# Attention and feed-forward on one core: the scores of the first seven head pairs as float32 products over six PSUM banks, first loads on two queues, a refitted transfer model

## The chip, the cores and the metric

The kernel runs on one core of a Trainium2 chip. The metric is the device time of one execution in microseconds (us), the median of three runs. Engines are named as in the profile: PE (TensorE, matrix products), DVE (VectorE), ACT (ScalarE), POOL (GpSimd) and SP (the queue from which nearly all transfers are issued). Each engine works through its own instructions strictly in the order in which the program lists them.

## The reference

Attention over 4 batches, 12 heads, 448 positions of 64 values, with scores capped at 30·tanh(s/30); its output, 1792 tokens of 768 values, goes through a feed-forward layer of width 2048. The feed-forward weights are handed over as 64-bit numbers and decoded on the chip.

```python
scores = scale * np.matmul(q, k.transpose(0, 1, 3, 2))
scores = cap * np.tanh(scores / cap)
attn = np.exp(scores - max);  attn = attn / (sum + 1e-09)
x = np.matmul(attn, v)              # -> 1792 x 768
h = x @ w_in                        # 768 x 2048
out = (h - np.tanh(h)) @ w_out      # 2048 x 768
```

## The kernel before

**Order.** A planner (class Plan) takes every operation with an estimated cost, the operations that it depends on and a due time, and simulates the engines and the transfer queues; the order that comes out is written down once, and each engine then follows it. So a constant of the planner changes no instruction, but it changes where instructions stand. `LEAD` and the `..._LAG` numbers say how early loads may be issued, `LANES`, `ISSUE` and the factors `slow` say what a transfer costs in the simulation.

**Attention.** Heads are taken in 24 pairs (6 per batch). A load of q or k brings two pairs (four transfers, 112 KB each; the very first pair is loaded alone), a stream transpose on DVE (L560) makes `qT` and `kT`, with the first head of a pair on partitions 0 to 63 and the second on 64 to 127. The scores of a pair are seven blocks of 128x448 (three per head, and one "tail" block whose 128 rows hold the last 64 rows of both heads). For the first `TILED_PAIRS` = 8 pairs k and q are split into a high and a low fp32r part (k: cast on ACT, L453, and difference on DVE, L464; q: scaled by `s8` on ACT, L583, difference on DVE, L588), and a block is three fp32r products, high·high, high·low, low·high (L745): a "visit" of PE makes the blocks of both heads, six products of 64 rows each, alternating between the two halves of the array; the tail takes three products of 128 rows from `kt`. All eight heads after that use "stacked" products of 128 rows (L710, 15 to a pair). Then ACT takes tanh out of PSUM (L755 or L718) and exp (L810).

The probabilities are multiplied with v (PV): for the first 11 pairs as float32 products (L889, 8 to a pair), which leave two records each in the trace. They accumulate in two banks of tag `s`; the denominators come out with them. To free a bank, DVE transposes the sums (`fsumT`, L921) and the rows are copied (`fnum`, L453 on ACT or L455 on DVE). Between two visits PE takes two or three PV products of the pair before.

**Feed-forward.** Five segments of chunks f (128 rows of weights each). In the first two segments each chunk's 64-bit weights are loaded (`w64`: two transfers of 384 KB, one of 768 KB), decoded on DVE in three passes (L1076, L1083, L1090) and written back decoded by POOL's queue for later segments. PE: L1222 to L1224 and L1275.

Batch 0's attention runs alone (to about 62 us); from then on attention and feed-forward chunks alternate on PE. PSUM has eight banks: `acc0` to `acc4`, two `s`, `h`.

**Start.** SP issues the cap's load, then k and q of the first pair and k and q of the second. A warm-up of 18 products on zeros runs on PE (L486). ACT loads its table for tanh at once (L1573).

Of the kernel before, what the change touches and what calls it, by code (L numbers as in the profile page):

```python
# [37 lines left out]
LEAD = (18000.0, 40000.0, 30000.0, 30000.0, 30000.0)  # L38

FREE_PAIRS = 8  # L40

TILED_PAIRS = 8
# [3 lines left out]
INSPECT_LAG, RAW_LAG, KEPT_LAG, V_LAG, QK_LAG = 15000.0, 3000.0, 3000.0, 3000.0, 1000.0  # L46
# [9 lines left out]
START = (1700.0, 2000.0, 3300.0, 1060.0, 2300.0)  # L56
# [7 lines left out]
GROUP = 3 * SCORE + 400.0  # L64
SCORES = 3 * GROUP + 3 * SCORE

SHIFT = 110.0

LANES = 8


BANKS = ["acc0", "acc1", "acc2", "acc3", "acc4", "s", "s", "h"]
# [247 lines left out]
class Build:  # L320
# [6 lines left out]
    def __init__(self, ctx, tc, q, k, v, w_in, w_out, out, consts, checks, general):  # L327
# [40 lines left out]
        for i in range(self.plan.tags["kt"]):  # L368
            t = self.cst.tile([128, 2, 2, self.TAIL], F32R, name=f"{nm}kt{i}")
            nc.gpsimd.memset(t.bitcast(F32)[:D, :, 1, :], 0.0)  # L370
            nc.gpsimd.memset(t.bitcast(F32)[D:, :, 0, :], 0.0)
            self.fixed["kt"].append(t)
# [20 lines left out]
        if not general:  # L393
            self.least, self.flagf, self.flag = checks
# [77 lines left out]
    def dma(self, eng, nbytes, fn, deps=(), alloc=(), uses=(), slow=1, long=False, key=1e18, lag=0.0):  # L472
        c = (650.0 if long else 550.0) if eng == "SP" else 600.0
        return self.plan.op(eng, c, fn, deps, alloc, uses, key, dma=nbytes * slow / 360.0, lag=lag)
# [4 lines left out]
    def warm_up(self):  # L479
# [8 lines left out]
        o = self.plan.op("D", 300.0, lambda: nc.vector.memset(z().bitcast(F32), 0.0), [], [z], key=-1e6)  # L488
        self.plan.op("PE", COLS[384] * WARM, fn, [o], [P], [z], key=-1e6)
# [3 lines left out]
    def fetch_qk(self, b, p, np_):  # L493

        nc, S = self.nc, self.S
        for nm, src in (("k", self.k), ("q", self.q)):
            raw = self.plan.buf(nm + "raw", [128, 2, S // 32, 32])
            ops = []
            for i in range(4):
# [3 lines left out]
                def fn(i=i, h=h, dh=dh, raw=raw, src=src):  # L503
                    nc.sync.dma_start(  # L504
# [6 lines left out]
                        "SP", np_ * S * 128, fn, [], [] if ops else [raw], [raw] if ops else [], slow=2.3,  # L511
                        lag=QK_LAG if (b, p) > (0, 1) else 0.0,
# [8 lines left out]
    def fetch_v(self, b, p):  # L521
# [4 lines left out]
        for hp in range(2):  # L526
            src = self.v[b, p + self.NP * hp]
            full, tail = (src[0:FULL], src[FULL:]) if hp == 0 else (src[TAIL:], src[0:TAIL])
            for part in range(2):

                def fn(hp=hp, part=part, full=full, tail=tail):
# [5 lines left out]
                    else:  # L537
# [6 lines left out]
                        [vr] if ops else [], slow=1.8, long=True, lag=V_LAG if (b, p) > (0, 0) else 0.0,  # L544
# [4 lines left out]
    def prep_pair(self, b, p):  # L549
# [3 lines left out]
        nc, S, D, F, TL, plan = self.nc, self.S, self.D, self.FULL, self.TAIL, self.plan  # L553
        T, tr = {}, {}
        for nm in ("k", "q"):
            raw, j, ops = self.raw_qk.pop((nm, b, p))
            t = T[nm] = plan.buf(nm + "T", [128, S])
            tr[nm] = self.dve(
                S,
                lambda t=t, raw=raw, j=j: nc.vector.transpose(t(), raw()[:, j].rearrange("p j a -> p (j a)")),  # L560
                ops, [t], [raw], extra=28,
            )
        if not self.tiled(b, p):
            return self.stack_pair(b, p, T, tr)
        kst, kt, qst = plan.buf("kst"), plan.buf("kt"), plan.buf("qst", [128, 2, S], F32R)
        kops = list(
            self.split(
                S, lambda: kst()[:, :S], lambda: kst()[:, S + TL :], T["k"], [tr["k"]], ([kst], []),
                ([T["k"]], [kst, T["k"]]),
            )  # L570
        )
        tops = []
        for h, c0 in ((0, F), (1, 0)):
# [3 lines left out]
                    2 * TL, lambda h=h, rows=rows: kt()[rows, :, h, :],  # L577
                    lambda rows=rows, c0=c0: self.pieces(kst(), rows, c0), kops,
                    [] if h else [kt], [kst, kt] if h else [kst], half=True,
                )  # L580
            )
        o1 = self.act(
            S, lambda: nc.scalar.activation(qst()[:, 0, :], T["q"](), AF.Copy, scale=self.s8), [tr["q"]],  # L583
            [qst], [T["q"]], aps=1,
        )
        o2 = self.dve(
            S,
            lambda: nc.vector.scalar_tensor_tensor(  # L588
                qst()[:, 1, :], T["q"](), self.s8, qst()[:, 0, :].bitcast(F32), op0=ALU.mult, op1=ALU.subtract
            ),  # L590
            [o1], [], [qst, T["q"]], extra=60,
        )
        self.ready[b, p] = dict(kst=kst, kt=kt, qst=qst, kops=kops, tops=tops, qops=[o1, o2])

    def tiled(self, b, p):
        return b * self.NP + p < TILED_PAIRS

    def pieces(self, kst, rows, c0):

        S, TL = self.S, self.TAIL  # L600
        t = kst[rows, c0 : c0 + S + 2 * TL].bitcast(F32)
        return t.rearrange("p (a b) -> p a b", b=TL)[:, 0 : S // TL + 2 : S // TL + 1, :]
# [73 lines left out]
    def s_banks(self, b, p, n):  # L676

        at = b * self.NP + p
        tags = ["s"]
        if b == 0:  # L680
            tags = ["acc0", "acc1", "acc2", "acc3", "acc4"]
        elif at < FREE_PAIRS:
            tags = ["acc0", "acc1", "s", "s"]
        self.s_rr = getattr(self, "s_rr", -1)
        out = []
        for _ in range(n):
            self.s_rr += 1
            out.append(self.plan.buf(tags[self.s_rr % len(tags)]))
        return out

# [32 lines left out]
    PRODUCTS = ((0, 0), (0, 1), (1, 0))  # L723

    def qk_group(self, b, p, c, dsts, e):
# [3 lines left out]
        heads = 2 if c < 3 else 1  # L729
        if not self.tiled(b, p):  # L730
            made = [self.stacked_block(b, p, h, c, e, dsts[h]) for h in range(heads)]
            return [t for ts, _ in made for t in ts], sum(cost for _, cost in made)
        ps = self.s_banks(b, p, heads)

        def fn():
            qst = r["qst"]()
            for n, (i, j) in enumerate(self.PRODUCTS):
                for h in range(heads):
                    rows = slice(D * h, D * h + D) if heads == 2 else slice(0, 2 * D)
                    c0 = 128 * c + self.TAIL * h  # L740
                    if heads == 2:
                        k = r["kst"]()[rows, (S + self.TAIL) * i + c0 : (S + self.TAIL) * i + c0 + 128]
                    else:
                        k = r["kt"]()[:, i].rearrange("p a b -> p (a b)")
                    nc.tensor.matmul(ps[h]()[:, :S], k, qst[rows, j, :], start=n == 0, stop=n == 2)  # L745

        cost = GROUP if heads == 2 else 3 * SCORE
        ks = "kst" if heads == 2 else "kt"
        o = self.pe(cost, fn, r["kops" if heads == 2 else "tops"] + r["qops"], ps, [r[ks], r["qst"]])
        ts = []  # L750
        for h in range(heads):
            new = e.users == 0
            ts.append(
                self.act(
                    S, lambda h=h: nc.scalar.activation(dsts[h](), ps[h]()[:, :S], AF.Tanh), [o],  # L755
# [874 lines left out]
```

## Time and profile before

| | |
|---|---|
| time, median of 3 runs | 704.82 us (702.48 to 705.82) |
| the profiled execution's own time | 704.72 us |
| its span in the trace | 702.9 us (1.8 us lie outside the span) |
| granted TensorE clock, mean | 0.988 |
| PE busy | 687.0 us, 98% |
| DVE busy / ACT busy | 534.6 us, 76% / 509.3 us, 72% |
| moved over DMA | 133.02 MB |

The span is what the rows are placed in: a start time in a row counts from its beginning. A granted clock of 1.00 is 2.4 GHz, 0.50 is 1.2 GHz; a value between is a mean over a stretch in which both occurred.

### The profile page before, as it was taken

To read this page: it belongs to the slowest core of one execution; us is meant where nothing else is said; L and a number is where in the kernel's file an instruction comes from. 1 tells how busy PE (TensorE), PEld (TensorE's weight loads), DVE (VectorE), ACT (ScalarE), POOL (GpSimd) and SP (SyncE) were. 2 spreads that over 40 slices of the span, in tenths; PEclk is the share of its full clock that TensorE was granted. 3 is DMA by queue.
4 is the path that set the end of the run, shared out by engine and by line. 5 is a ranking of instruction groups with operands and counts; after the bars stand their busy time and mean duration, and the time that the engine had idled before them with its cause. 6 is when DMAs were issued, how large, how long until landed. Compare 5 with 4: busy or idle time off the path is not lost.

```text
span 702.9 us, 10232 instructions
## 1 busy us (share of the span) xinstructions
PE 687.0 (98%) x3672; PEld 592.3 (84%) x3672; DVE 534.6 (76%) x849; ACT 509.3 (72%) x875; POOL 23.8 (3%) x51
## 2 busy tenths in 40 slices
PE   8999799998999999999999999999999999999997
PEld 6445487776998999999999989989999999999996
DVE  4798898998997989999899998899694343334333
ACT  5998585786985849587878998799685555554554
POOL 2011100110000000000000000000000000000000
PEclk9999899999999999999999999999999999999999
DMA  7999999899864729778767966595559445665523
GB/s 106 156 222 265 240 241 242 236 219 252 191 208 144 147 61 268 217 175 321 242 143 198 263 179 176 150 247 158 184 157 302 128 135 160 180 179 143 149 69 117
DMA packets 159516, 133.02 MB, mean 189 GB/s; under 512 B 115748, under 2 KB 144036, under 8 KB 159460
## 3 DMA queue, kind: packets, MB, share of 16 engines
q1 hardware_dynamic: 156228, 117.24, 66.2%
q0 software_dynamic: 3072, 14.94, 6.0%
q8 instruction: 31, 0.51, 0.3%
q14 instruction: 25, 0.20, 0.1%
q10 hardware_dynamic: 160, 0.13, 0.1%
HBM read 110.66 MB, written 21.63 MB: 188 GB/s over the span
## 4 chain that ended last, share of the span: by engine, by line
PE 89%; DVE 3%; DMA 3%; SPq 2%; ACT 1%; issue 0%; DVEq 0%
PE facc L1275 28%; PE fh L1222 11%; PE fh L1224 11%; PE fh L1223 10%; PE fs L889 8%; PE fs L710 6%; PE facc L745 3%; PE fs L1275 3%; PE fs L891 3%; PE fs L892 3%; PE fs L894 2%; DMA fw<-in_moe_w_in_dram 1%; SPq L504 1%; DMA fkraw<-in_k_dram 1%; DVE fsumT L921 1%; DMA fu<-fuk 1%
## 5 line engine op out<-in xcount | busy, mean ns | idle before, releaser
L1275 PE MATMUL facc<-fwo,fgh 128*128 128x512 f32 (+1 forms) x768 | 168.2, 341 | 0.0
L1275 PEld LDWEIGHTS facc<-fwo,fgh 128*128 128x128 f32 x768 | 124.2, 189 | 16.0 <-issue 2.2
L1222 PE MATMUL fh<-fxh,fwi 128*128 128x384 f32 x384 | 132.3, 345 | 0.1
L1224 PE MATMUL fh<-fxh,fwi 128*128 128x384 f32 x384 | 130.0, 338 | 0.0
L1223 PE MATMUL fh<-fxl,fwi 128*128 128x384 f32 x384 | 128.7, 335 | 0.0
L1275 PE MATMUL facc<-fwo,fgl 128*128 128x512 f32 (+1 forms) x384 | 98.9, 338 | 0.0
L1237 DVE TENSOR_TENSOR fg<-fh,fg 128x384 f32<-128x384 f32 x64 | 35.6, 556 | 62.3 <-ACT fg L1235 61.5
L464 DVE TENSOR_TENSOR fwi<-fu,fwi 128x768 fp32r<-128x768 f32 x66 | 62.7, 950 | 23.4 <-ACT fwi L453 23.0
L1222 PEld LDWEIGHTS fh<-fxh,fwi 128*128 128x128 f32 x384 | 72.1, 188 | 5.1 <-DVE fg L1237 1.3
L1223 PEld LDWEIGHTS fh<-fxl,fwi 128*128 128x128 f32 x384 | 72.2, 188 | 1.8 <-issue 0.9
L453 ACT CAST fwi<-fu 128x768 fp32r<-128x768 f32 x53 | 44.3, 836 | 39.1 <-PE fh L1224 31.3
L1224 PEld LDWEIGHTS fh<-fxh,fwi 128*128 128x128 f32 x384 | 72.0, 187 | 0.0
L464 DVE TENSOR_TENSOR fwo<-fu,fwo 128x768 fp32r<-128x768 f32 x66 | 62.9, 952 | 7.0 <-ACT fwo L453 6.7
L1275 PEld LDWEIGHTS facc<-fwo,fgl 128*128 128x128 f32 x384 | 59.0, 189 | 8.6
L1235 ACT ACTIVATE fg<-fh 128x384 f32<-128x384 f32 x64 | 31.4, 490 | 41.6 <-PE fh L1224 41.3
L718 ACT ACTIVATE fe<-fs 128x448 f32<-128x448 f32 x91 | 46.8, 542 | 13.6 <-PE fs L710 12.8
L453 ACT CAST fgh<-fg 128x384 fp32r<-128x384 f32 x62 | 31.7, 512 | 23.6 <-PE facc L1275 13.7
L710 PE MATMUL fs<-fqst,fkst 128*128 128x448 f32 x128 | 45.7, 377 | 3.1 <-ACT fnum L453 2.5
L810 ACT ACTIVATE fe<-fe,absc 128x896 f32<-128x896 f32 (+1 forms) x52 | 48.5, 952 | 0.3
L464 DVE TENSOR_TENSOR fel<-fe,feh 128x896 fp32r<-128x896 f32 x39 | 42.1, 1080 | 3.9 <-ACT feh L453 3.7
L464 DVE TENSOR_TENSOR fgl<-fg,fgh 128x384 fp32r<-128x384 f32 x64 | 35.2, 550 | 9.9 <-ACT fgh L453 9.3
L710 PE MATMUL fs<-fql,fkz 128*128 128x448 f32 x112 | 41.3, 368 | 0.0
(192 smaller groups left out, 1314.1 us busy)
## 6 DMA issues: line engine op xcount, KB each, us to landing
fu<-fuk SPq DMA_DIRECT2D x48, 768.0 KB
fw<-in_moe_w_in_dram SPq DMA_DIRECT2D x64, 384.0 KB
fw<-in_moe_w_out_dram SPq DMA_DIRECT2D x32, 768.0 KB
fuk<-fu POOLq DMA_DIRECT2D x16, 768.0 KB, 5.6
fkraw<-in_k_dram SPq DMA_DIRECT2D x44, 112.0 KB
fqraw<-in_q_dram SPq DMA_DIRECT2D x44, 112.0 KB
out_dram<-fo SPq DMA_DIRECT2D x12, 384.0 KB
fvraw<-in_v_dram SPq DMA_DIRECT2D x26, 96.0 KB
```

What stands on the lines that cost most here:

```text
L453: self.nc.scalar.copy(out(), in_())
L464: lambda: self.nc.vector.tensor_sub(lo(), x(), hi().bitcast(F32)),
L710: nc.tensor.matmul(ps()[:, :S], k, q, start=n == 0, stop=n == passes - 1)
L718: S, lambda: nc.scalar.activation(dst(), ps()[:, :S], AF.Tanh), [o],
L810: lambda e=e, w=w: nc.scalar.activation(e()[:, :w, :], e()[:, :w, :], AF.Exp, scale=self.absc),
L889: nc.tensor.matmul(out, va, e, start=n == 0, stop=n == 3)
L1222: nc.tensor.matmul(h()[:, :n], wh, ah, start=(d == 0), stop=False)
L1223: nc.tensor.matmul(h()[:, :n], wh, al, start=False, stop=False)
L1224: nc.tensor.matmul(h()[:, :n], wl, ah, start=False, stop=(d == ND - 1))
L1235: n, lambda: nc.scalar.activation(g()[:, :n], h()[:, :n], AF.Tanh), [prev], [g], [h], psum=True, key=k
L1237: o = self.dve(n, lambda: nc.vector.tensor_sub(g()[:, :n], h()[:, :n], g()[:, :n]), [o], [], [g, h], key=k + 600)
L1275: nc.tensor.matmul(banks[bk]()[:, c0 : c0 + ne], lhs()[:, ts], w()[:, k, e0 : e0 + ne], start=bk in firsts and bk not in begun, stop=stop ...
```

## The change

Seven of the eight tiled pairs (`JOINED` = 7) no longer split q and k. Their blocks are float32 products straight from the transposed tiles; the six blocks of both heads go in one visit into six banks (`SIX`), the tail follows in `acc0` later. The scale `s8` moves into the tanh. Pair 7 becomes a stacked pair. PV of these pairs takes its blocks in the order 0, 1, 2, 3 instead of 3, 0, 1, 2, and four PV products stand between visits.

```diff
+    def plain_pair(self, b, p):
+        q, k, kt = plan.buf("qst", [128, S]), plan.buf("kT", [128, S]), plan.buf("kt")
+        qo, ko = self.turn("q", b, p, q), self.turn("k", b, p, k)      # DVE transposes
+        for h, c0 in ((0, F), (1, 0)):                                  # kt: the tail rows of both heads
...
+                self.copy(
+                    TL, lambda h=h, rows=rows: kt()[rows, h, :], lambda rows=rows, c0=c0: k()[rows, c0 : c0 + TL],
+    def qk_full(self, b, p, es):
+        banks = [self.plan.buf(t) for t in SIX]
+            for c in range(3):
+                for h in range(2):
+                    rows, c0 = slice(D * h, D * h + D), 128 * c + self.TAIL * h
+                    nc.tensor.matmul(
+                        banks[2 * c + h]()[:, :S], r["k"]()[rows, c0 : c0 + 128], r["q"]()[rows], start=True, stop=True
+                    )
...
+                        lambda ps=banks[2 * c + h], e=e, h=h: nc.scalar.activation(
+                            e()[:, h, :], ps()[:, :S], AF.Tanh, scale=self.s8
+                        ),
-        order = (3, 0, 1, 2)
+        order = (0, 1, 2, 3) if self.joined(b, p) else (3, 0, 1, 2)
-                for _ in range((0, 3, 3, 2)[n]):
+                for _ in range(((4, 4) if self.joined(b, p) else (0, 3, 3, 2))[n]):
```

Of the first pair's eight loads four go to SP's queue and four to ACT's, and q comes ahead of k in every load of a group; the cap's load goes from SP's to POOL's queue; ACT's table load now stands behind its four issues.

```diff
-        for nm, src in (("k", self.k), ("q", self.q)):
+        for nm, src in (("q", self.q), ("k", self.k)):
+                eng = "A" if lead and hp else "SP"
-    nc.sync.dma_start(out=c, in_=cap.to_broadcast([128, 1]))
+    nc.gpsimd.dma_start(out=c, in_=cap.to_broadcast([128, 1]))
-    nc.scalar.activation(warm, warm, AF.Tanh)
```

The planner's numbers for transfers are set anew.

```diff
-LEAD = (18000.0, 40000.0, 30000.0, 30000.0, 30000.0)
+LEAD = (18000.0, 50000.0, 40000.0, 30000.0, 30000.0)
-INSPECT_LAG, RAW_LAG, KEPT_LAG, V_LAG, QK_LAG = 15000.0, 3000.0, 3000.0, 3000.0, 1000.0
+INSPECT_LAG, RAW_LAG, KEPT_LAG, V_LAG, QK_LAG = 15000.0, 3000.0, 3000.0, 3000.0, 2000.0
-LANES = 8
+LANES = 6
+SLOW = dict(qk=2.3, v=2.1, w_in=2.0, w_out=1.0, kept=1.35, keep=0.8, x=0.6)
```

The order that the planner writes moves with them. The first place is ACT's start; `facc0` to `facc4` and `fh` are banks, `fqst`, `fkst`, `fkt` and `fkT` the operands of the scores, `fel` and `feh` the probabilities. Before:

```order
L453 CAST fkst0_103<-fkT_6_167 128x448
L453 CAST fkt0_110<-fkst0_103 64x2x64
L583 ACTIVATE fqst_9_181<-fqT_8_178,s8_69 128x448
L453 CAST fkst1_105<-fkT_11_195 128x448
L755 ACTIVATE fel_14_207<-facc0_10_191 128x448
L810 ACTIVATE fel_14_207<-fel_14_207,absc_65 128x448
L755 ACTIVATE feh_18_224<-facc1_12_197 128x448
L755 ACTIVATE feh_18_224<-facc2_13_198 128x448
```

And after the change, behind the four issues and the table load:

```order
L455 COPY fkt0_109<-fkT_8_174 64x64 x2
L727 ACTIVATE feh_16_202<-facc0_9_180,s8_68 128x448
L727 ACTIVATE feh_16_202<-facc1_10_181,s8_68 128x448
L727 ACTIVATE fel_20_212<-facc2_11_182,s8_68 128x448
L805 ACTIVATE feh_16_202<-feh_16_202,absc_64 128x896
L750 ACTIVATE fel_21_219<-facc0_18_208,s8_68 128x448
L727 ACTIVATE fel_20_212<-facc3_12_183,s8_68 128x448
L727 ACTIVATE feh_24_227<-facc4_13_184,s8_68 128x448
L805 ACTIVATE fel_20_212<-fel_20_212,absc_64 128x896
L727 ACTIVATE feh_24_227<-fh_14_185,s8_68 128x448
```

Casts and scaling ahead of the first product are gone, and the last of the six banks is emptied behind seven tanh and two exp. On PE one visit of six products, the tail and three PV products now stand ahead of the second pair's visit, which takes all six banks again; before, 30 products of scores stood ahead of the first PV product.

The second place is on DVE, shortly after feed-forward has begun: around the transpose of a later pair's q (`fqT` from `fqraw`) and the sums (`fsumT`) whose transposes free the two `s` banks. Before:

```order
L455 CAST fwi_161_801<-fu_140_709 128x768
L955 TENSOR_TENSOR fx_163_807<-fnum_152_757,frb_159_794 128x384
L961 TENSOR_TENSOR fxt4_118<-fnum_152_757,frb_159_794 128x64
L560 STREAM_TRANSPOSE fqT_166_814<-fqraw_98_549 128x448
L464 TENSOR_TENSOR fwi_161_801<-fu_140_709,fwi_161_801 128x768
L464 TENSOR_TENSOR fxl_168_825<-fx_163_807,fxh_167_817 128x384
L1076 TENSOR_SCALAR fu_169_828<-fw64_122_641 128x1536
L464 TENSOR_TENSOR fwo_164_809<-fu_140_709,fwo_164_809 128x768
L1083 SCALAR_TENSOR_TENSOR fu_169_828<-fw64_122_641,fu_169_828 128x1536
L921 STREAM_TRANSPOSE fsumT_172_842<-fs_158_791 64x448
```

And after the change:

```order
L620 TENSOR_TENSOR fkst0_102<-fkT_152_650,fkst0_102 64x448
L457 CAST fxh_162_690<-fx_160_673 128x384
L573 STREAM_TRANSPOSE fqT_163_692<-fqraw_109_515 128x448
L932 STREAM_TRANSPOSE fsumT_164_698<-fs_149_641 64x448
L457 COPY fnum_166_708<-fs_149_641 64x448
L932 STREAM_TRANSPOSE fsumT_164_698<-fs_154_656 64x448
L466 TENSOR_TENSOR fxl_168_717<-fx_160_673,fxh_162_690 128x384
L1102 SCALAR_TENSOR_TENSOR fu_146_630<-fw64_104_498,fu_146_630 128x1536
```

The transpose still stands ahead of the sums, now directly; five rows that stood between them, the two decode passes of the next chunk among them, no longer do.

The third place is SP's queue, the loads that bring that q (`fqraw_98` before, `fqraw_109` after). Before:

```order
L504 DMA fqraw_98_549<-in_q_dram 32x28x32
L534 DMA fv1float322_300<-in_v_dram 128x3x64 x2
L536 DMA fv1float322_300<-in_v_dram 64x64 x2
L504 DMA fqraw_98_549<-in_q_dram 32x28x32 x2
L1033 DMA fw64_122_641<-in_moe_w_in_dram 64x6x128
L1046 DMA fw64_122_641<-in_moe_w_out_dram 128x768
L1033 DMA fw64_122_641<-in_moe_w_in_dram 64x6x128
L534 DMA fv1float320_186<-in_v_dram 128x3x64 x2
L536 DMA fv1float320_186<-in_v_dram 64x64 x2
L504 DMA fqraw_98_549<-in_q_dram 32x28x32
```

And after the change:

```order
L543 DMA fv1float322_261<-in_v_dram 64x64 x2
L1044 DMA fw64_104_498<-in_moe_w_in_dram 64x6x128 x2
L1058 DMA fw64_104_498<-in_moe_w_out_dram 128x768
L511 DMA fqraw_109_515<-in_q_dram 32x28x32 x4
L541 DMA fv1float320_195<-in_v_dram 128x3x64 x2
L543 DMA fv1float320_195<-in_v_dram 64x64 x2
L511 DMA fkraw_138_611<-in_k_dram 32x28x32 x4
```

The four parts of the load were spread over ten rows with a whole chunk of weights between them, and the last part came last; now the four are issued in one piece, ahead of the next chunk of weights.

## Rows read from the trace of the kernel before

**Rows 1.** The page, first part: busy time, share of the span, instructions.

```profile
PE 687.0 (98%) x3672; PEld 592.3 (84%) x3672; DVE 534.6 (76%) x849; ACT 509.3 (72%) x875; POOL 23.8 (3%) x51
```
**Rows 2.** Two stretches: length, busy us (instructions) of each engine, PEclk, DMA share, GB/s.

```profile
60.00:180.00 120.00, 112.96 (x496) 84.88 (x496) 107.80 (x156) 85.87 (x149) 10.95 (x18) 0.96 0.99 235
180.00:540.00 360.00, 359.79 (x1976) 327.97 (x1975) 322.16 (x503) 286.81 (x487) 3.20 (x6) 1.00 0.70 196
```
**Rows 3.** What PE waited for from 0 to 200 us: us in total, times, longest.

```profile
PE fs L745 <- DVE fsumT L921: 3.9, 1, 3.9
PE fs L710 <- ACT fnum L453: 2.5, 1, 2.5
```
**Rows 4.** PE's timeline at the middle stall: start, duration, operation, count, [idle before, releaser].

```profile
77.36 0.74 PE L745 MATMUL fs<-fqst,fkst 64*128 64x448 f32 x1 [3.87 <-DVE fsumT L921]
```
**Rows 5.** DVE's timeline over the same stretch.

```profile
71.26 0.65 DVE L560 STREAM_TRANSPOSE fqT<-fqraw 128x448 f32<-128x448 f32 x1 [2.59 <-DMA fv1float<-in_v_dram]
...
76.65 1.34 DVE L921 STREAM_TRANSPOSE fsumT<-fs 64x448 f32<-64x448 f32 x2
```
**Rows 6.** Short stretches, columns as in rows 2.

```profile
77.36:83.40 6.04, 6.03 (x27) 4.25 (x27) 5.64 (x11) 4.00 (x9) 0.64 (x1) 0.57 0.97 241
169.80:175.50 5.70, 5.70 (x23) 5.14 (x24) 5.55 (x9) 2.60 (x5) 0.00 (x0) 0.70 0.91 215
11.00:12.00 1.00, 1.00 (x8) 0.89 (x6) 0.90 (x3) 0.97 (x2) 0.00 (x0) 0.50 0.66 150
43.94:53.58 9.64, 9.64 (x38) 4.81 (x38) 9.13 (x16) 9.55 (x19) 1.84 (x3) 1.00 0.97 216
```
**Rows 7.** DVE's timeline at the late stall.

```profile
166.68 0.96 DVE L1076 TENSOR_SCALAR fu<-fw 128x1536 uint32<-128x1536 uint32 x1 [2.95 <-DMA fw<-in_moe_w_in_dram]
...
168.54 0.65 DVE L921 STREAM_TRANSPOSE fsumT<-fs 64x448 f32<-64x448 f32 x1
```
**Rows 8.** SP's timeline: an issue's start and duration.

```profile
64.51 0.58 SPq L504 DMA_DIRECT2D fqraw<-in_q_dram  x1
65.14 4.93 SPq L504 DMA_DIRECT2D fkraw<-in_k_dram  x1
...
156.62 2.01 SPq L1033 DMA_DIRECT2D fw<-in_moe_w_in_dram  x2
```
**Rows 9.** The start: timelines of SP, DVE and PE.

```profile
3.33 2.05 SPq L504 DMA_DIRECT2D fqraw<-in_q_dram  x4
...
7.73 0.65 DVE L560 STREAM_TRANSPOSE fqT<-fqraw 128x448 f32<-128x448 f32 x1
...
1.46 6.13 PE L486 MATMUL fs<-fxh 128*128 128x384 f32 x18 [1.46 <-DVE fxh L488]
9.22 0.44 PE L745 MATMUL facc<-fqst,fkt 128*128 128x448 f32 x1 [1.64 <-ACT fqst L583]
...
24.61 0.67 PE L745 MATMUL facc<-fqst,fkt 128*128 128x448 f32 x2 [0.32 <-DVE fqst L588]
```
**Rows 10.** DMA issues: count, KB each, median us from issue to landing.

```profile
fxk<-fxh POOLq DMA_DIRECT2D x6, 192.0 KB, 4.6
```
**Rows 11.** ACT's groups up to 70 us: busy us, mean ns, idle before.

```profile
L810 ACT ACTIVATE feh<-feh,absc 128x896 f32<-128x896 f32 x13 | 13.6, 1046 | 0.0
L755 ACT ACTIVATE feh<-facc 128x448 f32<-128x448 f32 x25 | 12.2, 544 | 0.0
...
L583 ACT ACTIVATE fqst<-fqT,s 128x448 fp32r<-128x448 f32 x8 | 5.3, 668 | 0.7 <-DVE fqT L560 0.6
```
**Rows 12.** PE's timeline: a visit, and float32 PV products in a row.

```profile
47.75 0.88 PE L745 MATMUL facc<-fqst,fkst 64*128 64x448 f32 x6
48.55 1.02 PE L889 MATMUL fs<-feh,fv1float 128*128 128x448 f32 x2
...
163.08 1.67 PE L889 MATMUL fs<-fel,fv1float 128*128 128x448 f32 x4
164.58 0.92 PE L889 MATMUL fs<-feh,fv1float 128*128 128x448 f32 x2
```

More of the change, by code (lines that the diff above doesn't have):

```diff
@@ L495, in fetch_qk @@
         nc, S = self.nc, self.S
-        for nm, src in (("k", self.k), ("q", self.q)):
+        lead = (b, p) == (0, 0) and not self.general
+        for nm, src in (("q", self.q), ("k", self.k)):
             raw = self.plan.buf(nm + "raw", [128, 2, S // 32, 32])
@@ L576, in prep_pair, with joined @@
                 self.copy(
-                    2 * TL, lambda h=h, rows=rows: kt()[rows, :, h, :],
-                    lambda rows=rows, c0=c0: self.pieces(kst(), rows, c0), kops,
-                    [] if h else [kt], [kst, kt] if h else [kst], half=True,
-                )
-            )
[L582 to L602, printed above, removed]
+                    TL, lambda h=h, rows=rows: kt()[rows, h, :], lambda rows=rows, c0=c0: k()[rows, c0 : c0 + TL],
+                    [ko], [] if h else [kt], [k, kt] if h else [k], half=True,
+                )
+            )
+        self.ready[b, p] = dict(k=k, kt=kt, q=q, kops=[ko], tops=tops, qops=[qo])
+    def joined(self, b, p):
+        return b * self.NP + p < JOINED and not self.general
     def stack_pair(self, b, p, T, tr):
@@ L674, in prep_v @@
         r.update(v1=v1, v2=v2, vops=list(o))
[L676 to L689, printed above, removed]
     def stacked_block(self, b, p, hp, c, e, dst):
@@ L721, in stacked_block @@
         return [t], cost
-    PRODUCTS = ((0, 0), (0, 1), (1, 0))
     def qk_group(self, b, p, c, dsts, e):
+        made = [self.stacked_block(b, p, h, c, e, dsts[h]) for h in range(2 if c < 3 else 1)]
+        return [t for ts, _ in made for t in ts], sum(cost for _, cost in made)
+    def qk_full(self, b, p, es):
         nc, S, D = self.nc, self.S, self.D
         r = self.ready[b, p]
[L729 to L733, printed above, removed]
-        def fn():
[L736 to L749, printed above, removed]
@@ L1506, in emit @@
         NP, NF = self.NP, self.NF
-        lead = NP * (SCORES + (8 * FULL32 if F32_PAIRS and not self.general else 22 * SCORE))
+        lead = NP * ((15 * SCORE if self.general else SCORES) + (8 * FULL32 if F32_PAIRS and not self.general else 22 * SCORE))
         chunk = 18 * COLS[384] + 9 * (COLS[512] + COLS[256])
@@ L1511, in emit @@
             f32 = max(0, min(NP, F32_PAIRS - b * NP)) if not self.general else 0
-            share[b] = sum(SCORES if self.tiled(b, p) else 15 * SCORE for p in range(NP)) + f32 * 8 * FULL32 + (NP - f32) * 22 * SCORE
+            share[b] = sum(SCORES if self.joined(b, p) else 15 * SCORE for p in range(NP)) + f32 * 8 * FULL32 + (NP - f32) * 22 * SCORE
         starts = [lead]
```

127 lines of the change are left out of this document (80 added, 47 removed).

## The prediction

> **What bounds the kernel now.** I read the page's busy shares first. PE is busy for 687.0 of 702.9 us [rows 1], so this kernel gets faster only where PE idles, runs at a lower clock, or is given less to do. The second view is the windows: from 180 to 540 us PE is busy for 359.79 of 360.00 us at clock 1.00, while from 60 to 180 us it is busy for 112.96 of 120.00 at 0.96, with the DMA engines at 0.99 of their time [rows 2]. So everything that can be won lies in the first 180 us, and in that part the transfers are as full as they can be.
>
> The third view is PE's list of waits. Two matter: 3.9 us for the sums' transpose, once, and 2.5 us for a copy of `fnum`, once [rows 3]. The first ends at 77.36 [rows 4]. The releaser named is DVE's transpose of the sums, which frees a bank `s`; but DVE was not busy, it stood. At 71.26 it began the transpose of a later pair's q after 2.59 us of waiting for a transfer, and the sums, which are behind it in DVE's order, were reached only at 76.65 [rows 5]. (The transfer named in that row is one of v; the operand is q, whose last part SP issued at 64.51 [rows 8].) The second works the same way: at 166.68 DVE had waited 2.95 us for a chunk's weights before decoding them, and the sums behind it came at 168.54 [rows 7]; those weights were issued at 156.62 [rows 8]. So the cause of both is a late transfer at the head of DVE's queue. SP's queue shows why it is late: an issue that takes 0.58 us when there is room takes 4.93 us right behind it [rows 8].
>
> A wait costs more than its length. In the 6.04 us after the first one the granted clock is 0.57, and 0.70 in the 5.70 us after the second, where PE otherwise runs at 1.00 [rows 6]. At full clock the same work would take 6.04 x 0.57 and 5.70 x 0.70 us: 2.6 and 1.7 us lost. With the 7.04 us of idle time from 60 to 180 us [rows 2], the supply of data costs 11.3 us of span in all, 6.5 of them (3.87 + 2.6) at the middle stall.
>
> At the start PE's warm-up runs from 1.46 to 7.59, its first product of scores comes at 9.22 after 1.64 us of idle time [rows 9], and the clock then falls to 0.50 for some time [rows 6].
>
> **The change, part by part.** *Scores, per pair.* A pair takes 9.64 us in the steady lead [rows 6]. A float32 PV product leaves two records, and four records take 1.50 us (163.08 to 164.58) [rows 12], so 0.375 a record and 0.75 a product; eight of these are 6.00, which leaves 3.64 for the scores of before: three visits of 0.80 (47.75 to 48.55) [rows 12] and the tail. After, the visit is six float32 products, so twelve records, on two halves of the array. No row shows float32 products on half of the rows, so I bound them. Rows of fp32r products show that the halves work at the same time: two of them start at 77.36 together [rows 4]. If the halves always overlap, twelve records take six slots of 0.375, 2.25 us; if never, 4.50 us. The program lists both records of the first head, then both of the second; if products start in the order listed, each head's second record runs beside the next head's first, and the twelve records take seven slots, 2.63 us. I take seven. Going to half rows and back costs something between nothing and the whole of a fp32r visit, 0.80; I take 0.45. So the visit is 3.08, with a tail of 0.75 the pair 3.83: +0.19 a pair, for the five pairs after the first two +0.95 us (six slots: -0.95; none beside another: +10.3). The Trainium skill's page "TensorE: Matmul & The Clock Gate", Part 3 (packing small matmuls), says that products of different row groups overlap and that starts and ends keep the queue's order; by that rule it is the seven slots, and by "TensorEngine Tiling (Array Packing)", Overview, up to twice the speed, the six, which would put the end at 693.1 instead of 695.0. Both speak against no overlap at all; the trace agrees with them for fp32r (the pair of rows at 77.36), and nothing in it shows float32.
>
> *Pair 7* goes from 21 products, six at a time in 0.80 us, to 15 of 128 rows. 15 products at what a third of a visit takes, 0.27, would be 4.0 us; the visit includes its switch, so they take less. Against 3.64 I take -0.4, with bounds of -0.8 and +0.4.
>
> *Work off PE.* Each joined pair drops a cast and a scaling on ACT and two differences on DVE; the tanh takes its scale from memory. The nearest row for such a scale, 0.668 us for the same shape, is 0.12 above a tanh's 0.544 [rows 11]: under 1 us for a pair's seven, less than the 0.668 and the cast that it drops. I put it at nothing: ACT does not end PE's waits in the lead, and has less to do. If that cover fails, it is 7 x 0.12 = 0.8 us a pair.
>
> *Start, first two pairs.* Before, the second load of four (q) was issued from 3.33 to 5.38 [rows 9], and its transpose began at 7.73; the scaling and the difference followed before PE could start. After, the two queues issue eight loads by about 3.3, one load's issue being 0.51 us (2.05 / 4). With the lead of before (issued by 5.38, transposed by 7.73, at most 2.35 us, some of it DVE's own queue) the transfers land at about 5.6 and two transposes of 0.65 follow: 6.9. DVE's small operations on the cap stand ahead of them, and the cap comes through POOL's queue now: a landing there takes 4.6 us [rows 10], so with an issue near 0.9 and about 0.8 for the small operations, 6.3, and 7.6 at worst for the transposes' end. The warm-up ends at 7.59 in any case. So the first product starts at about 7.5 instead of 9.22 without a gap, and the clock should not fall. Then a new wait comes: the second visit reuses all six banks, and ACT's order has seven tanh (0.544) and two exp (1.046) [rows 11] before the last is empty: 8.3 (first product done) + 5.9, with handovers about 15.0. To 15.0 come the visit 3.08 and six steps of 0.75 (five PV products, one tail): the third pair's scores start at 22.6. Before they were held until 24.61 [rows 9]. So -2.0 us, bounds -3.6 (no wait for the banks) and +1.
>
> *The transfers' order.* The q load that blocked DVE at 71.26 now stands behind less: summing the queue's rows, 10.45 MB go ahead of and with it before, 8.42 after. At the 235 GB/s of this stretch [rows 2] that is 8.6 us earlier. Its transpose stands behind 50.4 us of PE's work instead of 52.9, and PE is 2.0 us earlier by the start; 8.6 - 2.5 - 2.0 leaves 4.1, more than the 2.59 us that were missing. For the chunk at 166.68: 25.40 MB instead of 26.12, 3.1 us earlier, and its decode stands behind 149.5 us of PE's work instead of 137.3, 12.2 later; PE arrives 2.0 + 6.5 earlier, so 3.1 + 12.2 - 8.5 = 6.8 against the 2.95 missing. Between the last PV product into a bank `s` and its next use there are 1.8 to 2.7 us of other work on PE where there were 0.9 to 1.1, so a late DVE costs PE less. But a queue that was full stays full: the time saved pulls every demand forward by some 10 us against the same 235 GB/s, and by hand the DVE's arrivals at the transfers from 90 to 160 us are 0 to 7 us behind the landings. Some will wait. I leave 3 of the 11.3 us standing: -8.3 (bounds 0 and -11.3).
>
> *Sum.* 702.9 - 2.0 + 0.95 - 0.4 - 8.3 = 693.15 of span; with the 1.8 us outside it 694.95, **695.0 us**. The profiled execution (704.72) stands 0.1 under the median of 704.82, so nothing is added for that. A change of 0.5%, 3.5 us, is about what a measurement of this kernel tells from none.
>
> **Rivals.** (1) *The waits only move.* The DMA engines at 0.99 [rows 2] speak for it: the same bytes have to come before 160 us, and what PE wins at 73 us it gives back at the next chunk. Then -8.3 falls away: 703.3 us, no change. Against it: the two waits need only 2.6 and 3.0 us, and the blocking loads are 4 and 7 us better placed. (2) *Float32 products on half rows don't run beside each other.* The visit is then 4.50 + 0.45, 1.87 more than my 3.08, on seven pairs 13.1: 708.1 us, slower. It begins to turn the sign from 1.4 us more a visit (9.9 / 7). For it: no row shows the case; against it: the two halves start together in fp32r [rows 4]. (3) *All of it.* Six slots and no wait left: 695.0 - 1.9 - 3.0 = 690.1; with the start at its best bound 688.5.
>
> **How the numbers follow.** My own case (part of the waits gone, 692 to 699) 0.52; rival 3 0.18; rival 1 0.16; rival 2 0.09; a new wait that costs more than all of it saves 0.05. Faster by over 0.5% (under 701.3): 0.52, 0.18 and a little of rival 1, 0.73. Within it (to 708.3): most of rival 1, half of rival 2, 0.17. Slower: 0.10. The range from 688 to 704 leaves out rival 2 and the new wait, 0.14; the likeliest case's own range is 692 to 699.
>
> **What would show it.** Right: the first float32 product of scores by 7.7 us and no stretch at clock 0.50 behind it; a visit of about 3.1 us (2.7: six slots, 4.9: rival 2); a pair in the lead at 9.8 us; no wait of PE for sums near 75 and 170 us, and idle time of PE from 60 to 180 us of about 2 instead of 7.04. Wrong: new waits of DVE for weights between 90 and 180 us with PE's waits behind them and a clock under 0.9 after each; or a lead that ends later than 62 us.

## The result: 694.55 us, 1.3% faster

The changed kernel takes 694.55 us (median of 4 runs, 694.40 to 694.64), the kernel before 703.82 (4 runs in the same series, 702.48 to 705.82): a ratio of 0.9871 with a 95% interval of 0.9843 to 0.9900. The forecast was 695.0. The profiled execution has a span of 692.4 us at a mean clock of 1.00, where before has 702.9 at 0.988.

The first row is the page's busy shares of the changed kernel, the next two its windows (columns as in [rows 2]).

```profile
PE 681.7 (98%) x3617; PEld 585.0 (84%) x3617; DVE 522.1 (75%) x835; ACT 513.5 (74%) x866; POOL 22.3 (3%) x52
```

```profile
60.00:180.00 120.00, 118.89 (x539) 91.84 (x536) 116.27 (x169) 101.76 (x174) 8.79 (x16) 1.00 1.01 238
180.00:540.00 360.00, 358.30 (x1974) 327.04 (x1973) 312.91 (x491) 284.65 (x476) 3.19 (x6) 1.00 0.71 200
```

PE's busy time fell by 5.3 us [rows 1] and its idle time from 15.9 (702.9 - 687.0) to 10.7 (692.4 - 681.7), by 5.2: half of the gain is less or faster work, half is fewer waits. Between 60 and 180 us PE idles for 1.11 us instead of 7.04, at clock 1.00 instead of 0.96 [rows 2]. Some of it comes back: from 180 to 540 us there are 1.70 us of idle time where there were 0.21.

PE's waits up to 200 us, the three longest (against [rows 3]), and all of DVE's waits from 24 to 200 us:

```profile
PE fs L488 <- DVE fxh L490: 1.5, 1, 1.5
PE fs L900 <- ACT fel L805: 0.7, 1, 0.7
PE fs L687 <- ACT fel L695: 0.6, 1, 0.6
```

```profile
DVE fsumT L932 <- PE fs L900: 4.4, 3, 1.8
DVE fkt L457 <- PE facc L746: 2.5, 2, 1.8
DVE fqst L573 <- PE facc L746: 1.8, 1, 1.8
DVE fkT L573 <- PE fh L715: 1.1, 2, 0.9
DVE feh L457 <- ACT fe L805: 0.6, 1, 0.6
DVE fql L645 <- PE fs L687: 0.6, 1, 0.6
DVE fg L1249 <- ACT fg L1247: 0.2, 1, 0.2
```

Neither the wait for the sums nor that for `fnum` is there any more, and among DVE's waits none names a transfer; before, DVE waited 2.59 and 2.95 us for one at the two places [rows 5, 7].

The load of q that was late at the middle place, in SP's timeline, then its transpose and the sums in DVE's:

```profile
47.32 8.53 SPq L511 DMA_DIRECT2D fqraw<-in_q_dram  x4
```

```profile
67.51 0.64 DVE L573 STREAM_TRANSPOSE fqT<-fqraw 128x448 f32<-128x448 f32 x1
68.07 0.63 DVE L932 STREAM_TRANSPOSE fsumT<-fs 64x448 f32<-64x448 f32 x1
```

The last part of the load is issued by 55.85 instead of 65.09 [rows 8], and its transpose waits for nothing.

The start, in PE's timeline (against [rows 9]), and one pair of the steady lead (against [rows 12]):

```profile
7.27 2.15 PE L715 MATMUL facc<-fqst,fkT 64*128 64x448 f32 x9 [0.36 <-DVE fkT L573]
...
11.03 1.74 PE L900 MATMUL fs<-feh,fv1float 128*128 128x448 f32 x4 [0.29 <-issue]
...
14.44 2.14 PE L715 MATMUL facc<-fqst,fkT 64*128 64x448 f32 x9
...
21.60 2.14 PE L715 MATMUL facc<-fqst,fkT 64*128 64x448 f32 x9
```

```profile
31.02 2.15 PE L715 MATMUL facc<-fqst,fkT 64*128 64x448 f32 x9
32.63 0.54 PE L715 MATMUL fh<-fqst,fkT 64*128 64x448 f32 x1
33.00 0.54 PE L715 MATMUL facc<-fqst,fkT 64*128 64x448 f32 x1
33.01 0.54 PE L715 MATMUL fh<-fqst,fkT 64*128 64x448 f32 x1
33.47 1.77 PE L900 MATMUL fs<-feh,fv1float 128*128 128x448 f32 x4
...
40.44 2.14 PE L715 MATMUL facc<-fqst,fkT 64*128 64x448 f32 x9
```

The first product of scores starts at 7.27 instead of 9.22. The second pair's visit starts at 14.44, the third's at 21.60, where before the third pair's scores were held until 24.61. A pair takes 40.44 - 31.02 = 9.42 us instead of 9.64. The last records of a visit come two by two (33.00 and 33.01), 0.37 us after the two before (32.63): twelve records in six slots. The visit takes 33.47 - 31.02 = 2.45 us.

### The profile page after: what moved, and what is told of

Its sections match the earlier page's. It is cut to its first block, busy times and chain, and to the rows that moved or that the text cites. A ratio compares the mean times of both kernels' runs of the same rounds, so it can differ in the third digit from the quotient of the medians.

```text
span 692.4 us, 10096 instructions
## 1 busy us (share of the span) xinstructions
PE 681.7 (98%) x3617; PEld 585.0 (84%) x3617; DVE 522.1 (75%) x835; ACT 513.5 (74%) x866; POOL 22.3 (3%) x52
## 4 chain that ended last, share of the span: by engine, by line
PE 85%; DVE 8%; ACT 2%; DMA 2%; issue 1%; SPq 1%; ACTq 0%; DVEq 0%
PE facc L1287 26%; PE fh L1234 10%; PE fh L1236 10%; PE fh L1235 10%; PE fs L900 8%; PE fs L687 6%; PE fs L1287 3%; PE fs L902 3%; PE fs L903 3%; PE fs L905 2%; PE facc L715 2%; DVE fu L1102 1%; DVE fu L1095 1%; DMA fv1float<-in_v_dram 1%; DVE fwi L466 1%
## 5 line engine op out<-in xcount | busy, mean ns | idle before, releaser
L455 ACT CAST fwi<-fu 128x768 fp32r<-128x768 f32 x55 | 45.8, 834 | 30.0 <-PE fh L1236 26.4
L687 PE MATMUL fs<-fqst,fkst 128*128 128x448 f32 x136 | 48.0, 373 | 1.0 <-ACT fel L695 0.6
L455 ACT CAST fgh<-fg 128x384 fp32r<-128x384 f32 x58 | 29.7, 512 | 26.1 <-PE facc L1287 18.1
L687 PE MATMUL fs<-fql,fkz 128*128 128x448 f32 x119 | 43.5, 366 | 0.0
```

Of the source, the lines that this page charges most:

```text
L455: self.nc.scalar.copy(out(), in_())
L687: nc.tensor.matmul(ps()[:, :S], k, q, start=n == 0, stop=n == passes - 1)
```

## The experiments

The planner orders the whole program anew for nearly every edit, so a kernel's time holds the edit and what the new order does with it; only the first and the fourth leave every other instruction where it was. The kernel before scatters between 701.0 and 711.0 us over 61 runs in five series, the changed one by 0.24 us over 4 runs. Variants of the kernel before are held against the median of before in the same series, variants of the changed kernel against its 694.55 us. The changed kernel was timed in one series alone, and the medians of before differ by 1.2 us between series (703.82 to 705.04), so differences of about 1 us against 694.55 are not safe.

**1. Before, with two DVE instructions moved.** What do the two waits cost in place?

```diff
+MOVES = [('qT', 8, 'sumT', 5), ('u', 9, 'sumT', 10)]
+        todo = self.moved(best[1]) if near else best[1]
-        for o, e in best[1]:
+        for o, e in todo:
```

`moved` puts the DVE operation that fills the ninth `qT` (and the tenth `u`) behind the two transposes of the sums that it stood ahead of; PE, ACT, POOL and SP keep their orders.

> The kernel before with two DVE instructions moved and nothing else: the transpose of the q that came late at 71 us, and the first decode pass of the chunk that came late at 167 us, each now stand behind the transposes of the sums instead of ahead of them. My theory (a late transfer at the head of DVE's queue holds up sums that were ready): both of PE's waits and the low clock after them go, 6.5 + 4.2 us, of which some comes back where the q and the chunk are needed: a span of 692 to 696 us. Rival (the transfers bound the stretch, a wait only moves): 702 to 704 us, with a new wait of PE of 2 us or more behind each place.

700.84 us (before 704.10 in this series; ratio 0.9959, 0.9940 to 0.9978); span 699.9. DVE at the middle place, then PE at the late place in this kernel, then PE at the late place in the kernel before, and the longest of PE's waits in this kernel:

```profile
74.56 1.34 DVE L939 STREAM_TRANSPOSE fsumT<-fs 64x448 f32<-64x448 f32 x2
75.93 0.65 DVE L578 STREAM_TRANSPOSE fqT<-fqraw 128x448 f32<-128x448 f32 x1
```

```profile
166.43 0.91 PE L907 MATMUL fs<-feh,fv1float 128*128 128x448 f32 x2
...
173.02 0.35 PE L1240 MATMUL fh<-fxh,fwi 128*128 128x384 f32 x1
```

```profile
166.38 0.91 PE L889 MATMUL fs<-feh,fv1float 128*128 128x448 f32 x2
...
177.29 0.34 PE L1222 MATMUL fh<-fxh,fwi 128*128 128x384 f32 x1
```

```profile
PE fs L728 <- ACT fel L736: 1.9, 3, 0.7
...
PE fs L763 <- DVE fsumT L939: 1.0, 1, 1.0
PE fs L763 <- ACT feh L773: 1.0, 1, 1.0
PE fs L907 <- DMA fv1float<-in_v_dram: 0.9, 1, 0.9
```

The sums now run at 74.56 instead of 76.65 [rows 5] and the transpose of q behind them waits for nothing. At the late place the same products, from the PV pair to the start of the next chunk's, take 173.02 - 166.43 = 6.59 us instead of 177.29 - 166.38 = 10.91: 4.3 us, the wait of 2.50 and 1.8 of low clock. So both waits were what they were taken for, and the late one is priced as forecast (4.2). But the span is 3.0 us shorter, not 10: the list shows waits of 0.6 to 1.0 us in their place, for tanh to empty a bank, for the sums again, for v. Both theories are half right: the cause is DVE's queue, and most of what is won there is lost again nearby.

**2. Old scores, new numbers in the planner.** The kernel before with `LEAD`, `QK_LAG`, `LANES` and the transfer costs of the change.

```diff
-LANES = 8
+LANES = 6
-                        [vr] if ops else [], slow=1.8, long=True, ...
+                        [vr] if ops else [], slow=2.1, long=True, ...
```

> The kernel before (split fp32r scores, one queue at the start) with the planner's new numbers alone. My theory (the order of the transfers is what counts, and the new numbers make it): the q load that was late is issued earlier by 7.9 us of transfer time and the late chunk's decode stands behind 153 us of PE's work instead of 137; PE's waits between 60 and 180 us fall from 7.04 to under 2 us, span 693 to 697 us. Rival (the new order comes from the new scores, which need DVE and ACT less): waits as before, 701 to 704 us.

700.80 us (before 704.10; ratio 0.9963, 0.9937 to 0.9990); span 698.8. Its windows:

```profile
60.00:180.00 120.00, 119.53 (x541) 89.64 (x540) 116.76 (x168) 96.89 (x166) 10.53 (x18) 1.00 0.97 232
180.00:360.00 180.00, 177.29 (x969) 160.73 (x968) 162.60 (x240) 132.65 (x227) 3.20 (x6) 1.00 0.73 202
```

As my theory said, the idle time between 60 and 180 us is gone (0.47 us), but the time is not: 2.7 us of new idle time stand behind 180 us. The numbers alone are worth 3 us, not 8. The late q load is issued by 57.60 here and its transpose waits for nothing. Nothing was taken off DVE and ACT in this kernel, so the waits of the middle part can go without that.

**3. New scores, old numbers.** The reverse: the changed kernel with the old `LEAD`, `QK_LAG`, `LANES` and costs.

```diff
-LANES = 6
+LANES = 8
-LEAD = (18000.0, 50000.0, 40000.0, 30000.0, 30000.0)
+LEAD = (18000.0, 40000.0, 30000.0, 30000.0, 30000.0)
```

> The changed kernel with the planner's old numbers for transfers (lead times, lags, lanes, costs). My theory: scores and start keep their gain of about 4 us over before; the transfers are planned too early or too late again, some of the 8 us of waits and low clock comes back: 695 to 699 us of span. If the numbers alone made the order: 698 to 700 us. If the scores alone made it: 692 to 693.5 us.

(`START` and the cost of a visit, which belong to the new start and the new scores, keep their new values.)

694.83 us (694.09 to 695.04); span 693.1. SP's timeline at the q load, then DVE's:

```profile
62.89 2.00 SPq L511 DMA_DIRECT2D fqraw<-in_q_dram  x2
```

```profile
69.79 1.33 DVE L932 STREAM_TRANSPOSE fsumT<-fs 64x448 f32<-64x448 f32 x2
71.15 0.65 DVE L573 STREAM_TRANSPOSE fqT<-fqraw 128x448 f32<-128x448 f32 x1
```

Beside the new scores the numbers are worth 0.3 us, which the scatter of 1 us here does not tell from nothing. The last half of the q load is issued as late as before (until 64.89; before 65.09), but in this order the sums stand ahead of its transpose, PE's longest wait for the sums is 1.0 us instead of 3.9, and it idles for 2.35 us from 60 to 180 us instead of 7.04. So the gain does not hang on earlier transfers, by which the forecast explained the middle part: the planner gets around the late load by another order on DVE.

**4. A visit head by head.** Is it the alternation of the heads that makes the halves work side by side?

```diff
-            for c in range(3):
-                for h in range(2):
+            for h in range(2):
+                for c in range(3):
```

> The changed kernel with the six products of a visit listed as three of the first head, then three of the second (before: the heads in turn). If products start strictly in the order listed, only the last record of the first head runs beside the first of the second: 11 slots of 0.375 us instead of 6, a visit longer by 1.9 us, seven pairs 13 us: about 705 us of span. If the two halves of the array draw from the list apart from each other, the visit stays at 2.4 us and the span at 692 to 693 us.

700.71 us (700.59 to 700.81); span 698.8. A visit in PE's timeline:

```profile
23.45 2.63 PE L715 MATMUL facc<-fqst,fkT 64*128 64x448 f32 x10
...
26.76 0.64 PE L900 MATMUL fs<-feh,fv1float 128*128 128x448 f32 x1
```

The visit takes 26.76 - 23.45 = 3.31 us, 0.86 more, and 7 x 0.86 = 6.0 of the 6.2 us. Neither theory: 0.86 is 2.3 slots of 0.375, so 8.3 slots instead of 6 or 11. The single records of this visit form two rows and eight slots: one half starts records at 23.45, 23.93, 24.30, 24.68, 25.06 and 25.43, the other at 24.31, 24.79, 25.17, 25.54, 25.92 and 26.29; the last two of these are in bank `h`, which is the second head's. So the second head's first product, the fourth in the list, starts beside the second and 0.75 us ahead of the third: it is drawn forward past one product, but not past two.

**5. The start on one queue.**

```diff
-                eng = "A" if lead and hp else "SP"
+                eng = "SP"
-    nc.gpsimd.dma_start(out=c, in_=cap.to_broadcast([128, 1]))
+    nc.sync.dma_start(out=c, in_=cap.to_broadcast([128, 1]))
```

The table load at the kernel's beginning is back as well.

> The changed kernel with the start of before: all eight first loads and the cap on SP's queue, the table load at once. My step on the start says that the two queues bring the first product 1.7 us forward and keep the clock up: without them the first product starts at 8.5 to 9.2 us, and the span is 1.5 to 2.5 us longer, 694 to 695 us. Rival (the new scores need fewer steps before the first product, which is what brings it forward): less than 0.7 us.

695.96 us (695.88 to 696.18), 1.4 more. PE at the start:

```profile
7.75 2.14 PE L714 MATMUL facc<-fqst,fkT 64*128 64x448 f32 x9 [1.10 <-DVE fkT L572]
...
12.37 1.74 PE L899 MATMUL fs<-feh,fv1float 128*128 128x448 f32 x4 [1.15 <-DMA fv1float<-in_v_dram]
```

The first product starts at 7.75, only 0.48 later, so of the 1.95 us that it gained most is due to the shorter preparation. The first PV product waits for v until 12.37 (11.03 with two queues), but the second visit starts at 14.91 and the seventh at 59.75, 0.47 and 0.48 behind the changed kernel, so that wait costs nothing more. For the start the rival holds; the other 0.9 us of the 1.4 come behind the lead, in an order that the planner made anew.

**6. The work off PE put back.** Into each joined pair, without use:

```diff
+        o1 = self.act(S, lambda: nc.scalar.copy(s1(), k()), [ko], [s1], [k], key=self.at)
+        self.dve(S, lambda: nc.vector.tensor_sub(s1(), k(), s1()), [o1, ko], [], [s1, k], key=self.at)
+        o2 = self.act(S, lambda: nc.scalar.activation(s2(), q(), AF.Copy, scale=self.s8), ...)
+        self.dve(S, lambda: nc.vector.scalar_tensor_tensor(s2(), q(), self.s8, s2(), ...), ...)
```

> The changed kernel with the work that the split scores had off PE put back, to no use: for each of the seven pairs a copy and a scaling on ACT and two differences on DVE, of the same sizes as before, into a spare tile; nothing waits for them. After the third run the gain of 9 us can't come from the planner's new numbers. Theory now: DVE and ACT, relieved by some 18 us, reach the sums in time, so PE's waits go; with the work back some of them return: 695 to 699 us of span. Rival (it is PE's own order, one visit and the bank of the sums left alone for longer, that removes the waits): 692 to 693.5 us.

697.90 us (697.82 to 698.66), 3.4 more. PE's longest waits:

```profile
PE fs L911 <- ACT feh L816: 2.1, 1, 2.1
PE fs L698 <- ACT fqst L455: 1.7, 1, 1.7
```

The number lies in the range of the theory, but its reason does not hold: the waits for the sums do not return (0.2 us up to 200 us), and from 60 to 180 us PE idles for 1.64 us, where the changed kernel has 1.11 and before 7.04. Half of the loss is at the start: the first PV products wait 2.1 us for exp on ACT, and the second visit starts at 16.17 instead of 14.44, a lag of 1.7 us that the seventh still has (61.00 against 59.27). The second wait, for an operand cast on ACT, lies between 176 and 200 us.

**7 and 8. No joined pair, and six.** The others are stacked.

```diff
-JOINED = 7
+JOINED = 0      # run 8: JOINED = 6
```

> The changed kernel with none of the pairs joined: all 24 are stacked (15 fp32r products of 128 rows). By the price of PE alone a stacked pair is 3.1 us and a joined one 3.4 by the new trace, so PE has 2.3 us less to do; off PE each has about eight operations more on DVE and ACT. If PE's work alone counted: 690 us of span. Theory of relief: waits come back in the lead, 698 to 706 us.

> The changed kernel with six joined pairs: the seventh, which is the first beside feed-forward and takes all six banks there, becomes stacked. PE alone: 0.3 us less. If the visit over six banks beside feed-forward costs waits, up to 1 us more is won: 691 to 692.5 us of span. Theory of relief: DVE gets about eight operations more just where the sums were late at 75 us, and a wait of 1 to 3 us returns: 693.5 to 696 us.

None: 741.13 us (740.17 to 742.23); six: 702.51 us (701.38 to 702.85). First two windows of the kernel without joined pairs, then PE's waits of the one with six from 55 to 85 us:

```profile
0.00:60.00 60.00, 47.23 (x116) 27.30 (x117) 36.41 (x72) 39.08 (x64) 7.89 (x25) 0.80 0.99 186
60.00:180.00 120.00, 106.82 (x379) 70.40 (x378) 98.58 (x152) 84.16 (x144) 8.39 (x15) 0.90 0.74 176
```

```profile
PE fs L687 <- ACT fqst L455: 1.7, 1, 1.7
PE fs L687 <- ACT fel L695: 1.2, 2, 1.0
PE fs L687 <- DVE fsumT L932: 0.8, 1, 0.8
PE fs L687 <- DMA fv1float<-in_v_dram: 0.7, 1, 0.7
PE fs L687 <- ACT fnum L455: 0.6, 1, 0.6
```

Without joined pairs PE idles for 26 of its first 180 us, 12.8 of them in the lead, at a clock of 0.80 there: 46.6 us lost for 2.3 of PE's work saved. The one pair beside feed-forward costs 8.0 us when it is stacked. Its waits are for ACT, the sums and v, 5.0 us between 55 and 85 us where the changed kernel has 0.3.

Both edits move more than work. A stacked pair's scores go into the two banks `s` alone, which PV's sums use as well, where a joined pair has six others; without joined pairs no product of the first 60 us goes into `acc0` to `acc4` or `h`. How much of the two losses is the banks, and how much the operations more on DVE and ACT, these runs do not tell apart.

**9. Before, the seventh pair in other banks.** In the function that picks the banks:

```diff
-        if b == 0:
+        if at <= 6:
             tags = ["acc0", "acc1", "acc2", "acc3", "acc4"]
```

> The kernel before with one edit: the seventh pair, the first beside feed-forward, takes the banks acc0 to acc4 for its scores as the lead does, not acc0, acc1 and the two banks s that PV's sums hold. Theory now (what the change takes away in the middle is the need of this pair's scores for a bank s, whose sums DVE frees late): the 3.9 us wait at 77 us and the low clock behind it go or shrink, 698 to 701 us of span where before has 702.9. Rival (only DVE's and ACT's relief counts, the bank does not): 702 to 704 us.

700.67 us (before 705.04; ratio 0.9932, 0.9908 to 0.9957); span 700.5. DVE, then PE:

```profile
75.35 0.64 DVE L560 STREAM_TRANSPOSE fqT<-fqraw 128x448 f32<-128x448 f32 x1 [5.10 <-DMA fqraw<-in_q_dram]
...
79.69 1.32 DVE L921 STREAM_TRANSPOSE fsumT<-fs 64x448 f32<-64x448 f32 x2
```

```profile
80.38 2.17 PE L745 MATMUL fs<-fqst,fkst 64*128 64x448 f32 x6 [4.08 <-DVE fsumT L921]
```

The wait is there still, for the next pair that needs a bank `s`, with the same cause: DVE stood 5.10 us before a transpose of q whose transfer was late, and reached the sums at 79.69. The 2.4 us of span (4.4 between the medians) come from elsewhere in a new order. The span lies in the range of the theory of the bank, but its reason is not borne out here.

**10. After, with the banks s.** For the seventh pair's visit alone:

```diff
-        banks = [self.plan.buf(t) for t in SIX]
+        banks = [self.plan.buf(t) for t in (SIX if b == 0 else SIX[:4] + ["s", "s"])]
```

> The changed kernel with the mirror of that: the seventh pair's visit takes acc0 to acc3 and the two banks s instead of acc4 and h, so it has to wait for the sums of the pair before. Same work on every engine. If the bank s is what counts: a wait for the sums of 1 to 3 us ahead of this visit, span 693.5 to 696 us. If relief alone counts: 692 to 693 us.

700.28 us (699.17 to 701.12), 5.7 more. PE from 58 to 66 us:

```profile
61.33 1.77 PE L715 MATMUL facc<-fqst,fkT 64*128 64x448 f32 x8
...
65.04 1.02 PE L746 MATMUL facc<-fqst,fkt 128*128 128x448 f32 x2 [1.19 <-ACT feh L727]
```

The planner puts twelve products of feed-forward ahead of the visit, which starts at 61.33 (59.27 in the changed kernel) without the wait for the sums that the theory expected, and new waits follow, here for ACT's tanh. The kernel with these banks is slower; how much of that is the bank, and how much the order that the planner made for it, is not shown.

**11 and 12. Eight and nine joined pairs.**

```diff
-JOINED = 7
+JOINED = 8      # run 12: JOINED = 9
```

> The changed kernel with eight joined pairs. PE alone: 0.3 us more. Theory (the joined form pays where DVE is short, and the six-joined kernel lost 8 us): the eighth pair relieves DVE once more near 75 us, but its visit takes all six banks while feed-forward's first chunks need h: within 1.5 us of the changed kernel, 691.5 to 694 us of span. Rival (six banks beside feed-forward cost a wait): 695 to 698 us.

> The changed kernel with nine joined pairs, one more than the run with eight, which was 0.7 us faster than seven. PE alone: another 0.3 us more, and DVE and ACT are relieved once more. If relief goes on paying: 691 to 692 us of span. If the ninth pair, whose visit needs acc0 to acc4 and h among several chunks of feed-forward, has to wait for banks that feed-forward holds: 694 to 700 us.

693.87 us (693.61 to 694.15) and 692.93 us (692.70 to 693.24): 0.7 and 1.6 us under the changed kernel's 694.55. The ranges do not touch, but they come from three series, and the first difference is smaller than what the medians of before move between series. The window of nine from 60 to 180 us:

```profile
60.00:180.00 120.00, 119.99 (x545) 90.77 (x542) 112.82 (x167) 96.36 (x168) 9.31 (x16) 1.00 1.04 240
```

PE stands still for 0.01 us of this stretch. A visit over six banks between chunks of feed-forward costs no wait here, against the rival. Nine joined pairs have the lowest time measured here.

## Why the prediction was right, and where it was not

**The bound.** Right: what was won lies in the first 180 us, and as waits and low clock. A transfer late at the head of DVE's queue does hold the sums up (runs 1 and 9), and in the changed kernel DVE waits for no transfer from 24 to 200 us.

**The start**, -2.0 forecast. The third pair's scores begin at 21.60; before, their first product ran at 23.83 and the others were held until 24.61, so 2.2 to 3.0 us. The two queues give 0.5 of that (run 5). The wait for the six banks came as foretold, with the second visit at 14.44 instead of 15.0.

**The scores**, +0.95 forecast for five pairs. Here the term was wrong in sign: six slots, not seven, and 0.2 us for the change of form, not 0.45, so a visit of 2.45 us instead of 3.08 and 0.22 us less a pair (9.64 to 9.42), -1.1 for five. That products start strictly in the order listed was the assumption that failed; run 4 shows that PE takes one ahead of another.

**Pair 7**, -0.4, was not measured by itself; with it joined as well the time is 0.7 us lower (run 11), where PE's price alone says 0.3 higher; a new order is in that difference too.

**The work off PE**, put at nothing. A tanh with its scale from memory takes 0.635 us (ACT's rows for L727 up to 70 us) against 0.544 [rows 11], 0.6 us more for a pair's seven, less than the cast and the scaling that the pair drops, as foretold. But the work is not free at the start: put back, it delays the second visit by 1.7 us (run 6).

**The waits**, -8.3 forecast. The size came out nearly: at the sixth pair's scores (53.07 before, 49.85 after) start and scores had brought 3.2 us, so 7.3 of the 10.5 us of span come behind that, the seventh pair's 0.2 and whatever pair 7 gives among them. What the step foretold of the q load came too: it is issued 9.2 us earlier, its transpose waits for nothing, and DVE reaches the sums in time. The runs bear out the mechanism: the wait of 3.9 us is gone, or 1.0 us at most, where the sums do not stand behind a late transfer in DVE's queue, be it by hand (run 1), by an earlier load (run 2) or by another order on DVE (run 3), and it stays where they do (run 9, 4.08 us).

What the prediction had wrong is what the gain hangs on. It read the waits' end out of the order of SP's queue, "8.6 us earlier" for the q load. But beside the new scores a load as late as before costs 0.3 us (run 3), and beside the old ones the earlier load alone gives 3.3 of time (run 2). Relief of DVE and ACT is not needed for the waits to go either (run 2), and with the work put back the waits for the sums stay away (run 6). The new scores differ in how little is lost again elsewhere. Candidates are the banks, since a joined pair leaves `s` to the sums, and the order; runs 8 and 10 (8.0 us when the seventh pair is stacked, 5.7 us when it takes the banks `s`) fit the banks, but each has an order of its own, so this stays open.

The allowance of 3 us for waits that come back was too small for what a wait's removal does by itself: in run 1 4.6 of 7.6 us came back. (The late place gave 4.3. At the middle place the products from the visit's start to the next PV product took 10.4 us before, 73.02 to 83.39, and 7.1 in run 1, 73.78 to 80.87: 3.3.) In the changed kernel less came back: 1.1 us of idle time stand between 60 and 180 us, and 1.5 more than before from 180 to 540 us.

**The sum** came within 0.8 us of the span, in part by luck. Up to the sixth pair's scores the forecast gains 1.4 us (-2.0, and three pairs at +0.19) and the kernel gained 3.2; behind them it forecasts 8.3 (-8.3, -0.4, and two pairs at +0.19) and 7.3 came. The two errors partly cancel.

**The rivals.** "The waits only move" is wrong for the change but nearly right for runs 1 and 2, each worth 3 us. No overlap of float32 products is excluded by the pairs of records. "All of it" was right in the six slots, and too hopeful by 4 us in the time.

## What to carry to other kernels

An engine that is busy for 75% of the time can still hold up the busiest one, by what stands at the head of its queue; look there for the instruction that waits for a transfer, and for what stands behind it. But a wait that is taken out by reordering alone can give back much of its price nearby (4.6 of 7.6 us in run 1), so its length is not what it is worth. Nor is PE's own work the price of a form: the one with more matrix work and fewer side operations (9 joined pairs) beat the one with less matrix work by 48 us here, but it also had six other banks for its scores; before such a difference is put down to one of these, a run should change that one alone. Where a planner writes the order, hold changes of the work and of its numbers apart by running each with the other's old version, and look in each trace at the place in question: two orders can remove the same wait in two ways.

## What the runs showed of the hardware

Float32 products of 64 rows on the two halves of the array run side by side without loss when heads alternate: twelve records in six slots of 0.375 us, with 0.2 us for the change of form (2.45 - 2.25). The Trainium skill's page "TensorE: Matmul & The Clock Gate", Part 3 (packing small matmuls), says that starts keep the queue's order strictly. Six slots do not fit a list of two records for one product after the other, and in run 4 the fourth product of the list starts at 24.31, the third at 25.06, so here the measurement decides. For these products the sentence on engines at the head of this document, that each works strictly in the listed order, does not hold either.

Kernels on the old scores scatter from run to run: before by 10 us over 61 runs, runs 1, 2 and 9 by 3.8 to 4.5 over 9 or 10 runs each. Kernels on the new scores do so less, the changed kernel by 0.24 us and runs 11 and 12 by 0.54, over 4 runs each, most in runs 8 and 10 (1.5 us over 10 runs and 2.0 over 6). No run tells what causes it.
